# Making one more part of the first weights ahead of the first activation in a fused mLSTM and MLP kernel

## The chip, the cores and the metric

One NeuronCore of a Trainium2 chip runs the whole program; the other cores are idle. The metric is the device time of one execution in microseconds (us). Several executions of the same program are taken and their median is given.

## What is computed

The reference has two stages. The first is an mLSTM with 4 batches, 8 heads, 768 time steps and a head dimension of 40: a matrix state and a normaliser are carried along time with exponential input and forget gates, read out with the query, divided by a bounded norm and gated by a sigmoid. The second takes the result as 3072 rows of 320 features through an MLP with SiLU.

```python
h_tilde = np.einsum('bhde,bhe->bhd', C, qt)
denom = np.maximum(np.abs(nq), 1.0)
y[:, :, t] = o * h_tilde / denom
...
h = x @ w_in                      # [3072, 320] @ [320, 2048]
g = h * (1.0 / (1.0 + np.exp(-h)))
return (g @ w_out)                # [3072, 2048] @ [2048, 320]
```

The weights arrive as 64-bit floats.

## The kernel before, in words

**Units and steps.** Time is cut into 12 chunks of 64 steps and the batches into 2 pairs, which gives 24 units of 128 rows each. Three units make one step of the MLP (384 rows), so there are 8 steps (`Step`, L725). A step walks over 16 chunks of 128 hidden columns, `fc` = 0 to 15: `mm1(fc)` (L741) forms the hidden values in PSUM, `act(fc)` (L766) takes the tanh on ACT and the gate product on DVE, and `mm2(fc - 2)` (L797) adds to the three output tiles two chunks later (`LAG`). While one step runs, the attention work of the next three units is placed between its chunks: `block`, `close` and `turn` (L844 to L871) at the chunks given in `PLACES`.

**The weights.** They come in 20 parts (`Part`, L217), in the order that L319 writes out: c0 to c6 are tail weights (the last 64 input features, four chunks of columns each), i0 to i7 the other input weights (two chunks each), o0 to o7 the output weights (two chunks each). `load` (L225) issues one DMA on SP. `make` (L237) turns 64-bit words into 32-bit floats: two passes on ACT (L254, L255) and one on DVE (L256). `wmake(n)` (L331) makes the next n parts, and after each one issues the load of the next part not loaded yet. `halve` (L269) splits a tail part into a rounded part and a rest: two copies (L277) and two subtractions (L279), on ACT and DVE or, for c0, both on POOL. In step 0 `mm1(fc)` needs part i(fc // 2) and the halves of its tail part; its last two matmuls are those with the tail. `mm2(fc)` needs part o(fc // 2).

**What sets the order.** Each engine works through its own instructions in the order in which the program issues them. That order is written out by hand: a prologue (L896 to L983), then the chunks of step 0, each followed by the tuple of extra work in `FILL[fc]` (L984 to L1020). ACT, DVE and POOL take their shares of it in order, and SP issues its DMAs in order: eight hardware semaphores are used in turn, so a DMA waits until the eighth one before it has landed, and a load also waits until the buffer that it takes over was read for the last time (weights, q and k, and the rows of the MLP share the 11 buffers of the tag `big`).

**Around the change.** Before the first chunk the parts c0 and i0 are made, and c0 is halved on POOL. `FILL[0]` makes i1, adds the state of unit 2 (`state`, L659, matmuls), puts the states of units 1 and 2 into `Cm` on DVE (`carry`, L676: two copies L685 and two additions L693), finishes a part of the gates (L179, L180) and sends them to DRAM (`near`), and takes the exponent L422. `FILL[1]` makes o0 and takes the exponent of unit 3 (L393). `FILL[2]` makes i2, forms and weighs the scores of unit 3 (L523, L550), transposes gates (L194) and copies them (L204), loads unit 4 (v, k and o, D, lq), and prepares its mask on POOL (`shift`, L482). `FILL[3]` makes c2 and o1, halves c2 and adds the mask to D of unit 4 (L490); `FILL[4]` makes i3 and takes the exponent of D (L493); `FILL[5]` makes o2 and c4. At chunk 5 `block(3)` runs: unit 3 is read out, then normalised on DVE (L622 to L635) and scaled into `x` (L654); at chunk 6 `turn(3)` transposes it on PE (L709).

**PSUM.** The pool `psO` has three banks with the tag `o`. The states of units 1 and 2 (`pu`) and an exponent of unit 3 (`eq`) take them; the three output tiles of step 0 take them next, in `mm2(0)`. The hidden values use two banks of `psH`.

```python
order = "c0 i0 i1 o0 i2 c2 o1 i3 o2 c4 i4 o3 i5 o4 c6 i6 o5 i7 o6 o7"
def wmake(n):
    for p in parts[nmade[0] : nmade[0] + n]:
        p.make()
        wload(1)
    nmade[0] = min(nmade[0] + n, len(parts))
```

Of the kernel before, what the change touches and what calls it, by code (L numbers as in the profile page):

```python
# [43 lines left out]
def mlstm_mlp_kernel(  # L44
# [114 lines left out]
    def gates(lo, hi):  # L159

        init = NEG if lo == 0 else m_t[:, lo - 1 : lo]
        nc.vector.tensor_tensor_scan(
            m_t[:, lo:hi], f_t[:, lo:hi], i_t[:, lo:hi], init, op0=ALU.add, op1=ALU.max
        )
        yield
        l1 = max(lo, 1)
        tt = nc.vector.tensor_tensor
        tt(out=f_t[:, l1:hi], in0=f_t[:, l1:hi], in1=m_t[:, l1 - 1 : hi - 1], op=ALU.add)
        yield
        tt(out=f_t[:, l1:hi], in0=f_t[:, l1:hi], in1=m_t[:, l1:hi], op=ALU.subtract)  # L170
        nc.vector.tensor_scalar(f_t[:, l1:hi], f_t[:, l1:hi], -120.0, None, op0=ALU.max)
        if lo == 0:
            nc.vector.memset(f_t[:, 0:1], 0.0)
        yield
        nc.vector.tensor_tensor_scan(
            LF[:, lo:hi], pat[:, lo:hi], f_t[:, lo:hi], 0.0, op0=ALU.mult, op1=ALU.add
        )
        yield
        tt(out=i_t[:, lo:hi], in0=i_t[:, lo:hi], in1=m_t[:, lo:hi], op=ALU.subtract)  # L179
        tt(out=i_t[:, lo:hi], in0=i_t[:, lo:hi], in1=LF[:, lo:hi], op=ALU.subtract)  # L180
        yield
# [35 lines left out]
    class Part:  # L217
# [51 lines left out]
        def halve(self, eng=None, phases=(0, 1)):  # L269
            K, n, full = self.K, self.n, self.full  # L270
            for phase in phases:
                for k in range(2):
                    a, b = slice(k * K, (k + 1) * K), slice((1 - k) * K, (2 - k) * K)
                    cs = slice(k * n, (k + 1) * n)
                    hi = self.hi[a, :, cs]
                    if phase == 0:
                        eng.tensor_copy(hi, full[a]) if eng else nc.scalar.copy(hi, full[a])  # L277
                        continue
                    (eng or nc.vector).tensor_tensor(  # L279
                        out=self.hi[b, :, cs], in0=full[a], in1=hi.bitcast(F32), op=ALU.subtract  # L280
                    )
# [44 lines left out]
    def wload(n):  # L326
        for p in parts[nload[0] : nload[0] + n]:
            p.load()
        nload[0] = min(nload[0] + n, len(parts))
# [7 lines that stand above are left out]
# [536 lines left out]
    def run(n, it):  # L873
        for _ in range(n):
            next(it, None)

    u0, u1, u2, u3, u4 = units[:5]
# [29 lines left out]
    for _ in range(2):  # L907
# [5 lines left out]
    late = [gates(4 * L, 8 * L), gates(8 * L, S)]  # L913
# [67 lines left out]
    u2.xpose()  # L981
    u2.xput(st)
    u3.load_kvo()  # L983
    FILL = {  # L984
        0: lambda: (
            wmake(1),
            u2.state(),
            u1.carry(nc.vector.tensor_copy),
            u2.carry(),
            run(5, two),  # L990
# [2 lines left out]
        ),  # L993
        1: lambda: (wmake(1), u3.expo_act(), u3.near(), u4.load_qk()),
        2: lambda: (
            wmake(1),
            u3.scores(),
            u3.weigh(),
            run(2, near),
            u4.load_kvo(),  # L1000
            u4.load_d(),
            u4.load_q(),
            u4.shift(),
            u3.gate(),
            u3.keys(),
        ),
        3: lambda: (wmake(2), halve(2), u4.add(), run(1, late[0])),
        4: lambda: (wmake(1), u4.exp(), run(1, late[0])),
        5: lambda: wmake(2),
        6: lambda: (halve(4), wmake(2), run(1, late[0])),  # L1010
        7: lambda: (wmake(1), run(2, late[0])),
        8: lambda: (wmake(1), run(1, late[1])),
# [29 lines left out]
    for j in range(NSTEP):  # L1042
        st = steps[j]
        for fc in range(NFC):
# [28 lines left out]
            if j == 0:  # L1073
                FILL[fc]()

# [77 lines left out]
```

## Time and profile before

| | us |
|---|---|
| median of 3 runs | 451.97 |
| fastest and slowest run | 451.41, 453.16 |
| the profiled execution's own time | 454.21 |
| its span, from the first to the last instruction | 452.4 |
| PE busy (matmul) | 441.4 |
| DVE busy | 269.4 |
| ACT busy | 209.4 |
| POOL busy | 123.2 |

The profile is one execution taken by the hardware profiler. PE is the matrix engine (PEld its weight loads), DVE the vector engine, ACT the scalar engine, POOL the general engine, SP the engine that issues most of the DMAs (SPq its queue). A row of a timeline gives the start, the length, the engine, the line of the kernel, the operation, the output and the inputs by their names, their shapes and a count of merged instructions; in brackets stands how long the engine was idle before it and what released it. Matmuls are pipelined, so their lengths overlap a little.

### The profile page before, as it was taken

Reading aid. Unit: us, or ns where it says so; the run is one execution under the profiler, and the core shown is the slowest. Engines: PE = TensorE matmul, PEld = TensorE weight load, DVE = VectorE, ACT = ScalarE, POOL = GpSimd, SP = SyncE. Lnnn points to the kernel's source line nnn. Section 1 sums busy time; section 2 is a strip of 40 time slices with the busy share of each in tenths; the row PEclk is TensorE's granted clock in tenths of the full one; section 3 lists DMA queues with packets and bytes.
Section 4 is the critical chain, followed back from the end, with each engine's and each line's share of the span. In section 5 each row is a group of like instructions: output and inputs, shape, how many; then the busy total and the mean of one; then the engine's idle time right before and its main releaser. Section 6 shows DMA issues by size and latency. Waiting matters only on the chain.

```text
span 452.4 us, 11095 instructions
## 1 busy us (share of the span) xinstructions
PE 441.4 (98%) x4504; PEld 406.7 (90%) x4504; DVE 269.4 (60%) x595; ACT 209.4 (46%) x438; POOL 123.2 (27%) x134
## 2 busy tenths in 40 slices
PE   7989999999999999999999999999999999999996
PEld 4746577789999999999999999999999999999995
DVE  5765688768776655646646646646646555444442
ACT  7646456547446344354244354354354343334332
POOL 5821344222341322314323314313413230100000
PEclk9979999999999999999999999999999999999999
DMA  8999198414422514405403234315324110001001
GB/s 272 389 306 308 51 275 257 129 45 138 139 80 58 160 37 125 139 23 160 131 21 126 71 112 138 111 29 164 90 68 139 35 34 1 1 1 45 0 1 43
DMA packets 28691, 50.38 MB, mean 111 GB/s; under 512 B 3968, under 2 KB 15248, under 8 KB 28640
## 3 DMA queue, kind: packets, MB, share of 16 engines
q1 hardware_dynamic: 28288, 49.25, 35.2%
q8 instruction: 35, 0.57, 0.5%
q10 hardware_dynamic: 288, 0.34, 0.3%
q14 instruction: 16, 0.13, 0.1%
q0 software_dynamic: 64, 0.08, 0.1%
HBM read 45.65 MB, written 4.01 MB: 110 GB/s over the span
## 4 chain that ended last, share of the span: by engine, by line
PE 90%; DMA 5%; DVE 2%; ACT 1%; SPq 1%; issue 0%; ACTq 0%; DVEq 0%
PE ph L762 39%; PE pout L813 38%; PE p L609 3%; PE p L523 3%; PE pu L667 2%; PE p L594 2%; DMA wri<-in_w_in_dram 2%; PE p L709 2%; DMA vb<-in_vp_dram 1%; DMA qk<-in_qk_dram 1%; DVE wo L256 1%; PE pt L194 1%; SPq L438 0%; SPq L458 0%; SPq L235 0%
## 5 line engine op out<-in xcount | busy, mean ns | idle before, releaser
L769 ACT ACTIVATE th<-ph 128x384 f32<-128x384 f32 x128 | 62.5, 488 | 163.3 <-PE ph L762 160.9
L762 PE MATMUL ph<-xh,wh 128*128 128x384 f32 x336 | 115.4, 344 | 0.0
L783 DVE SCALAR_TENSOR_TENSOR th<-th,ph 128x384 f32<-128x384 f32 x112 | 62.1, 555 | 89.0 <-ACT th L769 88.4
L762 PE MATMUL ph<-xl,wh 128*128 128x384 f32 x336 | 113.7, 338 | 0.0
L813 PE MATMUL pout<-woh,gh 128*128 128x320 f32 x336 | 105.4, 314 | 0.0
L813 PE MATMUL pout<-woh,gl 128*128 128x320 f32 x336 | 103.9, 309 | 0.0
L813 PE MATMUL pout<-wol,gh 128*128 128x320 f32 x336 | 103.2, 307 | 0.0
L792 DVE TENSOR_TENSOR gl<-th,gh 128x384 fp32r<-128x384 f32 x112 | 65.6, 586 | 47.5 <-ACT gh L788 47.5
L788 ACT CAST gh<-th 128x384 fp32r<-128x384 f32 x112 | 57.5, 513 | 63.4 <-DVE th L783 62.7
L762 PE MATMUL ph<-xh,wl 128*128 128x384 f32 x224 | 75.9, 339 | 0.0
L813 PEld LDWEIGHTS pout<-woh,gh 128*128 128x128 f32 x336 | 63.0, 188 | 2.0
L687 POOL TENSOR_TENSOR Cm<-Cm,lq 40x328 f32<-40x328 f32 x40 | 30.1, 753 | 124.1 <-PE p L609 122.6
L762 PEld LDWEIGHTS ph<-xl,wh 128*128 128x128 f32 x336 | 63.1, 188 | 0.2
L762 PEld LDWEIGHTS ph<-xh,wh 128*128 128x128 f32 x336 | 63.1, 188 | 0.2
L813 PEld LDWEIGHTS pout<-woh,gl 128*128 128x128 f32 x336 | 63.0, 188 | 0.1
L813 PEld LDWEIGHTS pout<-wol,gh 128*128 128x128 f32 x336 | 63.1, 188 | 0.0
L507 POOL TENSOR_TENSOR qt<-qk,lq 104x512 f32<-104x512 f32 x22 | 29.2, 1326 | 121.5 <-ACT lq L503 114.9
L762 PEld LDWEIGHTS ph<-xh,wl 128*128 128x128 f32 x224 | 42.1, 188 | 0.0
L813 PE MATMUL pout<-wo,g 128*128 128x320 f32 x96 | 29.8, 448 | 2.9 <-DVE wo L256 2.9
L482 POOL TENSOR_TENSOR am<-mask,aT 128x512 f32<-128x512 f32 x20 | 24.3, 1215 | 9.3 <-DVE aT L204 7.8
L490 POOL TENSOR_TENSOR D<-D,am 128x512 f32<-128x512 f32 x20 | 25.8, 1289 | 2.2 <-DMA qk<-in_qk_dram 0.7
L550 DVE TENSOR_TENSOR D<-p,D 128x512 f32<-128x512 f32 x24 | 16.5, 689 | 16.3 <-PE p L609 11.3
(119 smaller groups left out, 494.9 us busy)
## 6 DMA issues: line engine op xcount, KB each, us to landing
qk<-in_qk_dram SPq DMA_DIRECT2D x24, 512.0 KB, 4.8
ko<-in_ko_dram SPq DMA_DIRECT2D x24, 320.0 KB, 4.5
wro<-in_w_out_dram SPq DMA_DIRECT2D x8, 640.0 KB, 7.0
D<-LFd SPq DMA_DIRECT2D x40, 128.0 KB, 3.1
lq<-LFd SPq DMA_DIRECT2D x40, 128.0 KB, 4.0
wri<-in_w_in_dram SPq DMA_DIRECT2D x8, 512.0 KB, 6.2
vb<-in_vp_dram SPq DMA_DIRECT2D x48, 82.0 KB, 4.5
out_dram<-ob SPq DMA_DIRECT2D x45, 80.0 KB, 2.1
```

What stands on the lines that cost most here:

```text
L482: nc.gpsimd.tensor_tensor(out=self.am, in0=mask.unsqueeze(1).broadcast_to([128, H, L]), in1=aT[:, self.c, self.p, :].unsqueeze(2).broadcas ...
L490: nc.gpsimd.tensor_tensor(out=self.Dm, in0=self.Dm, in1=self.am, op=ALU.add)
L507: nc.gpsimd.tensor_tensor(out=self.qt, in0=self.q[:KS], in1=self.lq[:KS], op=ALU.mult)
L523: nc.tensor.matmul(self.ps[d * L : (d + 1) * L, a * 4 + j, :], self.k[r, d * 4 + j, :], self.q[r, d * 4 + j, :], start=True, stop=True,)
L550: nc.vector.tensor_tensor(out=self.Dm, in0=self.ps, in1=self.Dm, op=ALU.mult)
L687: nc.gpsimd.tensor_tensor(out=v, in0=v, in1=self.lq[r, :, L - 1].unsqueeze(2).broadcast_to([D, H, D1]), op=ALU.mult,)
L762: nc.tensor.matmul(ph, w, x, start=(i == 0), stop=(i == len(ops) - 1))
L769: nc.scalar.activation(th, ph, AF.Tanh, scale=0.5)
L783: nc.vector.scalar_tensor_tensor(out=th, in0=th, scalar=1.0, in1=ph, op0=ALU.add, op1=ALU.mult)
L788: nc.scalar.copy(gh, th)
L792: nc.vector.tensor_tensor(out=gl, in0=th, in1=gh.bitcast(F32), op=ALU.subtract)
L813: nc.tensor.matmul(self.po[t], g[:, ts], w, start=(fc == 0 and i == 0), stop=(last and i == len(ops) - 1),)
```

## The change

One `wmake(1)` is put ahead of the tuple `FILL`, so that part i1 is made before the first chunk. The parts that follow stand one group earlier, up to o2: o0 in `FILL[0]`, i2 in `FILL[1]`, c2 and o1 with `halve(2)` in `FILL[2]`, i3 in `FILL[3]`, o2 in `FILL[4]`, c4 stays in `FILL[5]`. In `FILL[0]` the state of unit 2 goes ahead of the making, and in `FILL[2]` the scores and the weighing of unit 3 go ahead of it.

```diff
     u3.load_kvo()
+    wmake(1)
     FILL = {
         0: lambda: (
+            u2.state(),
             wmake(1),
-            u2.state(),
             u1.carry(nc.vector.tensor_copy),
...
         2: lambda: (
-            wmake(1),
             u3.scores(),
             u3.weigh(),
+            wmake(2),
             run(2, near),
             u4.load_kvo(),
             u4.load_d(),
             u4.load_q(),
             u4.shift(),
+            halve(2),
             u3.gate(),
             u3.keys(),
         ),
-        3: lambda: (wmake(2), halve(2), u4.add(), run(1, late[0])),
+        3: lambda: (wmake(1), u4.add(), run(1, late[0])),
         4: lambda: (wmake(1), u4.exp(), run(1, late[0])),
-        5: lambda: wmake(2),
+        5: lambda: wmake(1),
```

## Rows read from the trace of the kernel before

**Rows 1.** Busy time by stretches: stretch, length, busy (count) of each engine, clock, DMA.
```profile
60.00:70.00 10.00, 10.00 (x128) 7.45 (x127) 9.67 (x23) 5.02 (x11) 4.13 (x4) 1.00 0.99 287
...
300.00:400.00 100.00, 100.00 (x1057) 97.51 (x1056) 55.54 (x127) 41.64 (x88) 22.57 (x21) 1.00 0.20 60
```

**Rows 2.** Who waited for whom, 15 to 62 us: total, times, longest.
```profile
PE pout L813 <- DVE wo L256: 2.9, 2, 2.0
```

**Rows 3.** Timeline of PE, 20 to 80 us.
```profile
27.47 2.75 PE L813 MATMUL pout<-wo,g 128*128 128x320 f32 x6 [2.05 <-DVE wo L256]
...
39.20 0.62 PE L762 MATMUL ph<-xb,wh 128*128 128x384 f32 x2 [0.99 <-DVE wh L279]
...
49.73 1.88 PE L813 MATMUL pout<-wo,g 128*128 128x320 f32 x6 [0.85 <-DVE wo L256]
51.45 0.49 PE L709 MATMUL p<-ident,x 128*128 128x128 f32 x3
```

**Rows 4.** PE by half microseconds: stretch, length, busy (count), granted clock, DMA share, GB/s.
```profile
28.00:28.50 0.50, 0.50 (x3) 0.79 1.02 292
...
35.00:35.50 0.50, 0.50 (x4) 0.89 0.86 338
```

**Rows 5.** The chain that ended last, 27 to 62 us: start, length, what.
```profile
30.22 1.06 PE p L523 x32
...
31.85 3.46 PE ph L762 x6
...
57.16 1.61 PE pout L813 x6
58.78 1.64 PE ph L762 x6
60.42 0.62 PE p L523 x32
```

**Rows 6.** Timeline of ACT, 10 to 62 us.
```profile
21.13 0.49 ACT L769 ACTIVATE th<-ph 128x384 f32<-128x384 f32 x1 [1.82 <-PE ph L762]
...
24.10 0.80 ACT L254 ACTIVATE wro<-wro 128x640 f32<-128x640 f32 x1
24.79 0.75 ACT L255 ACTIVATE wro<-wro 128x640 uint32<-128x640 uint8 x1
...
35.34 0.49 ACT L769 ACTIVATE th<-ph 128x384 f32<-128x384 f32 x1 [7.47 <-PE ph L762]
...
41.57 0.61 ACT L493 ACTIVATE D<-D 128x512 f32<-128x512 f32 x1
```

**Rows 7.** Timeline of DVE, 10 to 62 us.
```profile
21.65 0.56 DVE L775 SCALAR_TENSOR_TENSOR g<-th,ph 128x384 f32<-128x384 f32 x1 [2.02 <-ACT th L769]
22.78 0.69 DVE L256 SCALAR_TENSOR_TENSOR wi<-wri 128x512 uint32<-128x512 uint32 x1 [0.57 <-ACT wri L255]
23.39 1.00 DVE L685 COPY Cm<-pu 40x328 f32<-40x328 f32 x2
24.40 1.00 DVE L693 TENSOR_TENSOR Cm<-Cm,pu 40x328 f32<-40x328 f32 x2
...
26.51 0.82 DVE L256 SCALAR_TENSOR_TENSOR wo<-wro 128x640 uint32<-128x640 uint32 x1
...
46.82 0.68 DVE L654 SCALAR_TENSOR_TENSOR x<-ko,p 128x256 f32<-128x256 f32 x3
...
48.46 1.21 DVE L256 SCALAR_TENSOR_TENSOR wo<-wro 128x640 uint32<-128x640 uint32 x1
```

**Rows 8.** Timeline of SP, 0 to 80 us: the issue of i1.
```profile
10.75 0.43 SPq L235 DMA_DIRECT2D wri<-in_w_in_dram  x1
```

**Rows 9.** DMA issues of SP, 10.7 to 11 us (i1): count, KB, us to landing.
```profile
wri<-in_w_in_dram SPq DMA_DIRECT2D x1, 512.0 KB, 5.9
```

**Rows 10.** Timeline of POOL, 0 to 62 us: the additions to D of units 4, 5.
```profile
33.84 1.27 POOL L490 TENSOR_TENSOR D<-D,am 128x512 f32<-128x512 f32 x1
...
47.72 1.28 POOL L490 TENSOR_TENSOR D<-D,am 128x512 f32<-128x512 f32 x1
```

## The prediction

> **What bounds the kernel now.** I read the busy time by stretches first: from 60 us to 400 us PE is busy for the whole of each of the eight stretches, so a microsecond that PE gets back before 60 us reaches the end of the program, unless a feeder of PE falls behind later [rows 1]. Next comes the list of waits between 15 and 62 us: PE waited for the making of output weights (the vector step of `make`, L256) twice, 2.9 us in all [rows 2]. The timeline of PE puts the places: 2.05 us before the first group of the second product (`mm2(0)`, parts o0), 0.99 us inside `mm1(4)` before its two matmuls with the tail weights (c2), and 0.85 us before `mm2(4)` (o2) [rows 3]. Last the granted clock in stretches of half a microsecond: PE runs at 2.4 GHz until it stands still, resumes, and then falls to 1.2 GHz, from 28.0 to 28.5 us on until between 35.0 and 35.5 us [rows 4]. The chain shows what that costs: the groups of 27 to 35 us take nearly twice what the same groups take later [rows 5].
>
> Why o0 is late is read on ACT and DVE, which work in the order of the program. o0 passes through ACT behind the tanh of chunk 1 [rows 6]; its step on DVE (26.51 us) stands behind i1, two copies and two additions of `carry`, and the gate of chunk 1 [rows 7].
>
> **The change part by part.** No instruction is added or taken away; seven parts and one `halve` change place.
>
> i1 ahead of the first activation: two ACT passes and one DVE pass. The passes on ACT took from the end of the first tanh (21.13 + 0.49) to 22.78, where DVE started: 1.16 us; DVE took 0.69 us [rows 6, 7]. Their cover is the hole before that tanh: ACT idle 1.82 us, DVE idle 2.02 us before the first gate [rows 6, 7]. 1.16 us fits ACT's hole, and DVE would end about 0.2 us before the gate is ready: cost nothing. The cover is gone if i1's bytes are late: issued at 10.75, landed 5.9 us later, 16.65 us; ACT is free for it from 21.13 - 1.82 = 19.31 on [rows 6, 8, 9]. Spare: 2.6 us.
>
> o0 one group earlier: ACT now gives it the place of i1, behind the tanh that ends at 21.62. Its two passes took from 24.10 to 25.54 us, 1.44 us, so they end near 23.1 [rows 6]; DVE needs 0.82 us, so o0 is ready near 23.9 instead of 27.33 [rows 7]. PE comes to `mm2(0)` at 27.47 - 2.05 = 25.42 us [rows 3]. **This stall, 2.05 us, goes.** What is late next there are the PSUM banks: the second and third tile of `mm2(0)` take the banks that the copies and additions of `carry` read, and these now stand behind o0. They took 1.0 and 1.0 us, from 23.39 to 25.40 [rows 7], so the copies end near 24.9 and the additions near 25.9; PE wants the second bank near 25.42 + 0.54 = 26.0 and the third near 26.5 (a third of 1.61 each). The banks are free in time, the third by 0.6 us.
>
> The clock: with no standstill at 25.4 us I take the fall to 1.2 GHz as gone. `mm2(0)` took 2.75 us [rows 3] against 1.61 in full clock, the scores of unit 3 took 1.06 against 0.62, `mm1(3)` 3.46 against 1.64 [rows 5]: 1.14 + 0.44 + 1.82 = **3.40 us**. The 0.57 us of small transposes between the scores and `mm1(3)` I leave out; halved they would be 0.28 more.
>
> c2, o1 and `halve(2)` one group earlier: in the kernel before, the tail was ready 39.2 - 35.34 = 3.9 us after the tanh that it follows [rows 3, 6]. It now follows the tanh of chunk 2, which comes near 25.9 us (PE ends `mm1(2)` at 25.42 and ACT still has i2 and the exponent of unit 3), so it is ready near 30 to 31, the weighing of unit 3 and the copies of `near` included. PE wants it after `mm2(0)`, scores, transposes, `mm1(3)`, `mm2(1)` and four matmuls of `mm1(4)`: 25.4 + 1.6 + 0.6 + 0.4 + 1.6 + 1.6 + 1.1 = 32.3 us. **The 0.99 us go.**
>
> o2 from group 5 to group 4: its DVE step took 1.21 us at 48.46, behind the chain of normalising unit 3, whose x was written from 46.82 [rows 7]. In group 4 it stands ahead of that chain, and several microseconds ahead of `mm2(4)`. **0.85 us go**, and the group that followed took 1.88 us where a fed one takes 1.61 [rows 3, 5]: 0.27 more.
>
> The DMA queue of SP: the order becomes o2, unit 4's q and k, c4, i4, then v, k/o, D and lq of unit 4. Two loads, 256 and 512 KB, pass ahead of those; at the 292 to 338 GB/s beside the clock rows [rows 4] that is 2.3 to 2.7 us for what stands behind. The one that matters is D: POOL added the mask from 33.84 to 35.11, ACT took the exponent at 41.57 [rows 6, 10], 6.5 us spare, and PE now arrives about 6.4 us earlier (2.05 + 3.40 + 0.99). So ACT may stand still for up to 2.7 us there. PE feels it only through the x of unit 3, written from 46.82 and transposed at 51.45 [rows 3, 7]: 4.6 us less its own 0.68, less the 1.12 of the o2 stall, leaves 2.8 us. Cost nothing, with little to spare at the worst end. Moving u2.state ahead of the making changes no engine's order, as one is all PE and the other has none: nothing.
>
> One contention has to be weighed. DVE's making of o2 took 1.21 us against 0.82 for o0, and POOL's addition ran from 47.72 to 49.00 over its first half [rows 7, 10]. The halving of c2 on DVE now falls where POOL starts the mask of unit 4. If POOL went first, the wait is at most one POOL addition, 1.28 us, and the tail would be ready at 32.3 at worst, just when PE wants it: I take no cost, 0.5 us as the bound. The Trainium skill, SBUF — State Buffer, section Who interferes with whom, says that a DVE instruction with two SBUF inputs and a GpSimd one that reads SBUF exclude each other, the second blocking fully; by that rule the order of issue decides here, and the 1.21 us row agrees with it only in part, since DVE is recorded as started before POOL ended.
>
> The sum: 2.05 + 3.40 + 0.99 + 0.85 + 0.27 = 7.56 us. The profiled execution took 454.21 us for a span of 452.4; by it the new one is 446.65. The median of the runs shown is 2.24 us lower, so I set the same gain against it: 451.97 - 7.56 = 444.41, call it **444.4 us**.
>
> **The rivals.** (a) The clock did not fall in the runs behind the median. For: the median is 2.24 us under the profiled execution. Against: the runs lie within 1.75 us, less than the 3.40 us at stake, so they are likely all of one kind, and the one trace has the fall. Then only the waits go: 451.97 - 4.16 = 447.8 us. The Trainium skill, TensorE: Matmul & The Clock Gate, Part 1, says the watch on PE's activity runs free of the kernel's start, so slow matmuls can differ between executions; no run here shows it.
>
> (b) A new wait in the old one's place: the banks of `mm2(0)`. For: o0's 0.82 us stands ahead of the carries on DVE now, and the third bank comes free only 0.6 us before PE asks for it. Against: every row from which that is worked out is a plain duration of this stretch. If the carries ended 1.5 us later, PE would stand about 1 us and, if the clock fell again, keep the 3.40: 444.4 + 1.0 + 3.4 = 448.8 us.
>
> (c) Slower: the exponent of unit 4 holds up ACT. c4 and i4 wait on SP for the buffers of i1 and o0, and D of unit 4 queues behind them. Each microsecond that D is later than 2.8 us beyond now costs one on PE, so the kernel gets slower from 2.8 + 7.6 = 10.4 us on; at 12 us it takes 453.6. Against: both buffers are released near 24 us, and the queue needs 2.3 to 2.7 us for the bytes.
>
> (d) One of the two later waits stays (the tail by the contention, or o2): 444.4 + 0.5 to 1.1, up to 445.5, inside the forecast's own range.
>
> **How the numbers follow.** Forecast with (d) 0.66, (a) 0.22, (b) 0.07, (c) 0.03, and 0.02 for no change. The range: below, the transposes (0.28) and, by my estimate, as much as 0.8 us of short restarts that the sum leaves out: 443.3. Above, to the upper edge of (a): 448.2. That leaves out (b), (c), no change and part of (a). A measurement of this kernel tells about 0.5% from no change, 2.3 us: faster means under 449.7. The forecast, (a) and (b) lie there: 0.95; no change 0.02, a late D that eats only the gain 0.01: 0.03 the same; the rest of (c) 0.02 slower.
>
> **What would show it.** Right: PE has no idle over half a microsecond between 24 and 50 us; the granted clock stays full through 28 to 35 us; o0's DVE step lies ahead of the carries, near 23 us; `mm2(0)` starts near 25.4 us and lasts about 1.6; unit 3's x is transposed near 44 us instead of 51.45. Wrong: a wait of PE for `carry` or its additions at 26 us; a clock of half between 28 and 35 us with no wait; ACT idle before the exponent of unit 4 for more than 3 us with PE idle behind it; or PE gaps after 60 us, which would say that the gain is given back later.

## The result and the profile after

The changed kernel takes 446.93 us (median of 4 runs, 446.67 to 449.48) against 452.57 us for the kernel before in the same comparison (4 runs, 451.41 to 453.43): a ratio of 0.989, interval 0.9846 to 0.9934. It is faster by 5.6 us where 7.6 was forecast (444.4 us); 446.93 lies inside the range, nearer to rival (a), 447.8, than to the forecast.

The profiled execution of the changed kernel is the slowest of the four: 449.48 us, span 447.7. Its timeline of PE answers to [rows 3] and [rows 5].

```profile
20.03 1.53 PE L762 MATMUL ph<-x,wi 128*128 128x384 f32 x4 [1.01 <-DVE wi L256]
...
25.93 1.78 PE L813 MATMUL pout<-wo,g 128*128 128x320 f32 x6
27.63 0.69 PE L523 MATMUL p<-qk 40*64 40x64 f32 x32
28.26 0.42 PE L194 MATMUL pt<-ident,home 32*64 32x32 f32 x8
28.61 1.56 PE L762 MATMUL ph<-x,wi 128*128 128x384 f32 x4
...
31.97 1.45 PE L762 MATMUL ph<-x,wi 128*128 128x384 f32 x4
32.97 0.81 PE L762 MATMUL ph<-xb,wh 128*128 128x384 f32 x2
...
42.67 1.78 PE L813 MATMUL pout<-wo,g 128*128 128x320 f32 x6
44.29 0.49 PE L709 MATMUL p<-ident,x 128*128 128x128 f32 x3
```

None of the three waits is left: `mm2(0)` at 25.93, the tail matmuls at 32.97 and `mm2(4)` at 42.67 follow their predecessors without a bracket. From the start of chunk 0 to the transposition of unit 3's x (L709) it is 44.29 - 20.03 = 24.26 us, where [rows 3] and the same start, 19.19 us, give 51.45 - 19.19 = 32.26. I call this length **the stretch**; all experiments are read on it. The granted clock stays full in it. By half microseconds, and then by stretches from 60 us on (columns as in [rows 1]):

```profile
28.00:28.50 0.50, 0.50 (x32) 0.43 (x23) 0.50 (x2) 0.50 (x2) 0.00 (x0) 1.00 1.04 410
...
35.00:35.50 0.50, 0.50 (x3) 0.34 (x2) 0.29 (x1) 0.50 (x2) 0.17 (x1) 1.00 1.11 260
```

```profile
60.00:70.00 10.00, 9.97 (x127) 7.28 (x126) 9.78 (x15) 7.39 (x14) 4.42 (x5) 1.00 0.96 291
70.00:80.00 10.00, 9.44 (x62) 6.73 (x61) 9.70 (x22) 5.16 (x10) 4.18 (x4) 1.00 0.53 146
80.00:90.00 10.00, 10.00 (x39) 7.70 (x38) 4.13 (x9) 3.50 (x7) 0.00 (x0) 0.83 0.08 26
```

Of the 8.0 us won in the stretch, about 2.5 went again between 70 and 90 us: PE is idle for 0.56 us, and behind it the clock is at half speed (1.2 GHz) from 80.4 to 83.9 us, 0.83 on average from 80 to 90. That is this one execution; the other three took 446.67 to 446.94. DVE in the stretch answers to [rows 7], POOL and ACT to [rows 10] and [rows 6].

```profile
23.82 0.83 DVE L256 SCALAR_TENSOR_TENSOR wo<-wro 128x640 uint32<-128x640 uint32 x1 [0.79 <-ACT wro L255]
24.56 1.00 DVE L685 COPY Cm<-pu 40x328 f32<-40x328 f32 x2
25.59 1.02 DVE L693 TENSOR_TENSOR Cm<-Cm,pu 40x328 f32<-40x328 f32 x2
...
30.77 1.59 DVE L279 TENSOR_TENSOR wh<-wtc,wh 64x256 fp32r<-64x256 f32 x2
```

```profile
30.93 1.15 POOL L482 TENSOR_TENSOR am<-mask,aT 128x512 f32<-128x512 f32 x1 [5.14 <-DVE aT L204]
35.33 1.28 POOL L490 TENSOR_TENSOR D<-D,am 128x512 f32<-128x512 f32 x1 [3.24 <-DMA D<-LFd]
```

```profile
36.64 0.63 ACT L493 ACTIVATE D<-D 128x512 f32<-128x512 f32 x1 [0.56 <-POOL D L490]
```

o0's step on DVE now stands ahead of the carries; the carries end at 26.61 us and PE does not wait for their banks. The halving of c2 takes 1.59 us instead of 0.87 beside POOL's mask, and ends at 32.36, 0.6 us before PE comes to it. D of unit 4 comes later (POOL waits 3.24 us for the DMA) and ACT stands still for 0.56 us.

### The profile page after: what moved, and what is told of

Its sections match the earlier page's. It is cut to its first block, busy times and chain, and to the rows that moved or that the text cites. A ratio compares the mean times of both kernels' runs of the same rounds, so it can differ in the third digit from the quotient of the medians.

```text
span 447.7 us, 11095 instructions
## 1 busy us (share of the span) xinstructions
PE 439.7 (98%) x4504; PEld 406.3 (91%) x4504; DVE 273.8 (61%) x595; ACT 209.6 (47%) x438; POOL 123.3 (28%) x134
## 4 chain that ended last, share of the span: by engine, by line
PE 87%; DVE 4%; DMA 4%; ACT 2%; issue 1%; SPq 1%; DVEq 0%; ACTq 0%
PE ph L762 39%; PE pout L813 37%; PE p L609 3%; PE p L523 3%; PE pu L667 2%; PE p L594 2%; DMA qk<-in_qk_dram 2%; PE p L709 1%; DMA wro<-in_w_out_dram 1%; DMA ko<-in_ko_dram 1%; DVE wi L256 1%; DVE wo L256 1%; DVE home L175 0%; PE pt L194 0%; DVE xl L721 0%
## 5 line engine op out<-in xcount | busy, mean ns | idle before, releaser
L762 PE MATMUL ph<-x,wi 128*128 128x384 f32 x64 | 24.1, 501 | 1.0 <-DVE wi L256 1.0
```

The lines of the kernel that those rows point to most:

```text
L762: nc.tensor.matmul(ph, w, x, start=(i == 0), stop=(i == len(ops) - 1))
```

## The experiments

Three runs repeat the two kernels as they are (e1, e2, e12). One fills the first wait of the kernel before (e4), four put parts of the change back (e5 to e8), and four try for more (e3, e9 to e11). The table has all kernels. "Full clock" are the executions whose mean granted clock is 0.998 or more; the stretch is that of the one traced execution. The median of the kernel before depends on how many of its executions lost the clock: over all timed executions it is 453.50 us, and the gain of the change 6.6 us.

| kernel | runs | median, us | at full clock: runs, median | stretch, us |
|---|---|---|---|---|
| before (with e1) | 67 | 453.50 | 28, 452.06 | 32.26; e1 30.64 |
| e4 standstill filled | 12 | 452.88 | 10, 452.29 | 29.78 |
| e5 only the front part | 10 | 449.94 | 8, 449.80 | 26.65 |
| e8 o0 late | 6 | 448.67 | 4, 448.38 | 25.77 |
| e7 tail late | 12 | 449.47 | 8, 448.22 | 25.52 |
| e6 o2 late | 6 | 448.11 | 5, 448.10 | 25.37 |
| after (with e2, e12) | 16 | 446.93 | 15, 446.92 | 24.26, 24.25, 24.25 |
| e3 | 6 | 446.99 | 6, 446.99 | 24.24 |
| e9 | 6 | 447.27 | 6, 447.27 | 24.25 |
| e10 | 6 | 447.30 | 5, 447.12 | 24.24 |
| e11 | 6 | 447.54 | 4, 447.24 | 25.79 |

**e1, the kernel before once more, no edit.**

> The kernel before, unchanged, to see the mean granted clock of every run. Theory: every run falls to 1.2 GHz after the standstill before the first group of the second product, as the traced one did (about 7 us at half clock, mean clock 0.99); times 451.4 to 453.5. Rival: the fall is in the traced execution alone, the timed runs show a mean clock of 1.00, and the gain of the change in them holds no clock.

453.04 us (12 runs) against 453.61 (23 runs of the same kernel), ratio 0.999, 0.9965 to 1.0016. Neither what was expected (every execution falls) nor its rival (only the traced one) holds. Its trace has the three waits at the same size, but the clock came back sooner. PE timeline, then PE by microseconds:

```profile
28.04 2.83 PE L813 MATMUL pout<-wo,g 128*128 128x320 f32 x6 [2.04 <-DVE wo L256]
...
38.16 0.62 PE L762 MATMUL ph<-xb,wh 128*128 128x384 f32 x2 [1.00 <-DVE wh L279]
```

```profile
28.00:29.00 1.00, 0.96 (x3) 0.70 (x4) 0.96 (x2) 0.46 (x2) 0.00 (x0) 0.89 1.00 258
29.00:30.00 1.00, 1.00 (x3) 0.67 (x2) 0.00 (x0) 0.00 (x0) 0.00 (x0) 0.50 0.90 212
...
32.00:33.00 1.00, 1.00 (x10) 0.79 (x11) 0.97 (x3) 0.00 (x0) 0.00 (x0) 0.91 1.04 311
```

Half speed lasts about 3.4 us here and about 7 us in the trace of before [rows 4], after the same wait. Each execution's mean clock shows which kind it was: the profile's list of cores gives, for before, e1 and e4 in this order,

```profile
core 0: 452.4 us, clock 0.991
```

```profile
core 0: 451.4 us, clock 0.996
```

```profile
core 0: 451.5 us, clock 1.000
```

So the 67 timed executions of the kernel before can be sorted by it, into three groups: 28 at 0.998 or more, median 452.06 us (450.97 to 453.86); 16 at 0.995 or 0.996, 453.52 (452.77 to 455.63); 23 at 0.994 or less, 454.93 (453.81 to 456.99). **The clock falls in 39 of 67 executions and stays full in 28, and a whole fall costs 454.93 - 452.06 = 2.9 us** (95% by resampling: 2.5 to 3.4). The mean does not say where in an execution the clock fell. That the place is the wait before `mm2(0)` is seen in the two traces; for the others it is taken over from them.

**e2 and e12, the changed kernel once more, no edit.**

> The changed kernel, unchanged. Theory: the timed runs lie at 446.7 to 447.0 with a mean clock of 1.00; the 2.5 us more of the traced execution are the fall of the clock at 80 to 84 us that follows the new wait of PE at 78 us, and come in some executions only. The start of the first chunk (20.03 against 19.19 us) varies with the landing of a load and is not the change's. Rival: the late start and the wait at 78 us are in every execution.

> The changed kernel once more, on the same chip as the three others, for comparison: 447 to 447.5 by the last time, and the stretch from the first chunk to the transposition of unit 3's x at 24.25 us by every theory. The start of the first chunk: 19.2 to 19.8 us if DVE's making of i0 starts ahead of POOL's subtractions, 20.0 to 20.8 if behind them.

447.39 us (6 runs, ratio 0.9866, 0.9832 to 0.9900) and 446.48 (6 runs, ratio 0.9857, 0.9825 to 0.9890). Fifteen of the sixteen executions of the changed kernel are at full clock. Neither trace has the 0.56 us wait or the half clock at 80 us. Where the first trace parts from e2's is this pair of rows on DVE and POOL:

```profile
65.61 1.43 DVE L171 TENSOR_SCALAR home<-home 32x256 f32<-32x256 f32 x1
```

```profile
65.60 1.30 POOL L507 TENSOR_TENSOR qt<-qk,lq 104x512 f32<-104x512 f32 x1 [4.49 <-DVE home L170]
```

DVE's instruction, started 10 ns after POOL's, took 1.43 us; in e2 it started 0.18 us ahead of POOL's and took 0.28. A second one followed, beside POOL's next row: the scan L175 took 1.22 us where e2's took 0.67. DVE has few holes there, so the last gates (L180) ended at 78.05 instead of 77.48 us and PE waited until 78.11, with the clock down behind it. That was in 1 of 16 executions, if the mean clock is taken as its mark.

In e12, D of unit 4 comes later than in the first trace, and ACT waits longer for it. Its rows on ACT and PE:

```profile
38.05 0.63 ACT L493 ACTIVATE D<-D 128x512 f32<-128x512 f32 x1 [2.03 <-POOL D L490]
```

```profile
20.01 1.53 PE L762 MATMUL ph<-x,wi 128*128 128x384 f32 x4 [0.99 <-DVE wi L256]
...
44.26 0.49 PE L709 MATMUL p<-ident,x 128*128 128x128 f32 x3
```

The stretch is 24.25 us all the same: 2.03 us of ACT cost PE nothing. In e3, where nothing in the stretch differs from the changed kernel, ACT waited 3.09 us, the most of all traces, and the stretch is 24.24.

**e4, the kernel before with its first wait filled with matmuls that no result uses.**

```diff
+            if j == 0 and fc == LAG:
+                warm(9, psU.tile([128, 512], F32, tag="u", name="fill"))
             if fc >= LAG and (j, fc) != (NSTEP - 1, NFC - 1):
                 st.mm2(fc - LAG)
```

> The kernel before with nine bf16 matmuls (128 x 512, into a free bank, results unused) put on PE between the first product of chunk 2 and the first group of the second product, where PE stood still for 2.05 us. All the waits stay. Theory: the standstill is what brings the clock down; without it PE runs at 2.4 GHz through 28 to 35 us, and the time is 3.0 to 3.6 us under the kernel before, about 449. Rival: the clock falls all the same, or had not fallen in the timed runs: 452 to 453, no difference.

452.88 us (12 runs), ratio 0.9988, 0.9961 to 1.0014. PE timeline and the clock in the place where before ran at half:

```profile
26.81 2.12 PE L890 MATMUL fill<-maskb,identb 128*128 128x512 bf16 x9
28.93 1.88 PE L813 MATMUL pout<-wo,g 128*128 128x320 f32 x6
...
35.08 1.45 PE L762 MATMUL ph<-x,wi 128*128 128x384 f32 x4
38.30 0.62 PE L762 MATMUL ph<-xb,wh 128*128 128x384 f32 x2 [1.77 <-DVE wh L279]
```

```profile
31.00:32.00 1.00, 1.00 (x41) 0.89 (x31) 0.50 (x1) 0.00 (x0) 0.00 (x0) 1.00 0.99 250
```

The fill takes the place of the wait, the clock stays full, and `mm2(0)`, scores and `mm1(3)` are at the short durations. But PE now comes earlier to the tail weights, which ACT and DVE have not moved, and waits 1.77 us for them instead of 0.99. So 0.78 us of what full clock gives are paid back at once, and the stretch is 32.26 - 29.78 = 2.48 us shorter than in the traced execution of before, near the 2.9 us (2.5 to 3.4) between the groups. The time near 449 that was expected did not come, since the median of the kernel before holds many executions that never lost the clock. At full clock e4 and before are alike (452.29 and 452.06); the fill makes full clock more frequent, 10 of 12 against 28 of 67. Two of the twelve fell all the same.

**e5, only the front: i1, o0 and i2 earlier; c2, o1 and o2 where they were.**

```diff
             u3.weigh(),
-            wmake(2),
...
-            halve(2),
...
-        3: lambda: (wmake(1), u4.add(), run(1, late[0])),
+        3: lambda: (wmake(2), halve(2), u4.add(), run(1, late[0])),
...
-        5: lambda: wmake(1),
+        5: lambda: wmake(2),
```

> Only the front of the change: i1 ahead of the first chunk, o0 and i2 one group earlier; c2, o1, the halving of c2, i3 and o2 back in their old groups. Measured from the start of the first chunk to the transposition of unit 3's x, which the changed kernel does in 24.25 us and the kernel before with its standstill filled in 29.78. Theory (each wait has its own price): the first wait and the fall of the clock stay away, the waits for the tail (1.0 to 1.8 us) and for o2 (0.85 and 0.27 us) come back: 26.4 to 27.2 us, 2.2 to 2.9 us slower than the changed kernel. Rival (one chain through ACT and DVE sets the pace, and the waits only hand the same loss on): the two later waits swallow the first one's gain, 29 us or more, 5 us slower than the changed kernel.

449.94 us (10 runs), ratio 0.9921, 0.9889 to 0.9953. PE timeline:

```profile
33.82 0.62 PE L762 MATMUL ph<-xb,wh 128*128 128x384 f32 x2 [1.00 <-DVE wh L279]
...
44.34 1.88 PE L813 MATMUL pout<-wo,g 128*128 128x320 f32 x6 [0.85 <-DVE wo L256]
46.06 0.49 PE L709 MATMUL p<-ident,x 128*128 128x128 f32 x3
```

The two later waits are back at the sizes of [rows 3]; the stretch is 26.65, 2.40 us more than after. The runs at full clock put it at 449.80 - 446.92 = 2.9 us (2.3 to 3.5 by resampling).

**e6, o2 alone late; e7, c2, o1 and the halving alone late; e8, o0 alone late.**

```diff
# e6
-        4: lambda: (wmake(1), u4.exp(), run(1, late[0])),
-        5: lambda: wmake(1),
+        4: lambda: (u4.exp(), run(1, late[0])),
+        5: lambda: wmake(2),
```

```diff
# e7
-            wmake(2),
...
-            halve(2),
...
-        3: lambda: (wmake(1), u4.add(), run(1, late[0])),
-        4: lambda: (wmake(1), u4.exp(), run(1, late[0])),
+        3: lambda: (wmake(2), halve(2), u4.add(), run(1, late[0])),
+        4: lambda: (wmake(2), u4.exp(), run(1, late[0])),
```

```diff
# e8
             u2.state(),
-            wmake(1),
             u1.carry(nc.vector.tensor_copy),
...
-        1: lambda: (wmake(1), u3.expo_act(), u3.near(), u4.load_qk()),
+        1: lambda: (wmake(2), u3.expo_act(), u3.near(), u4.load_qk()),
```

> The changed kernel with o2 back in group 5, made together with c4 behind the normalising of unit 3. Theory: the wait of 0.85 us before the second product of chunk 4 comes back and nothing else: 25.2 to 25.5 us on the same stretch, 1.1 us slower than the changed kernel. Rival: with the waits before it gone, PE reaches that group with the same lag to DVE and the wait is over 1.5 us, or it is hidden and under 0.3 us.

> The changed kernel with c2, o1 and the halving of c2 back in group 3 (i3 then stands with o2 in group 4). Theory: the wait inside the first product of chunk 4 comes back with 1.0 to 1.8 us: 25.3 to 26.2 us on the same stretch, 1.0 to 1.9 us slower than the changed kernel. Rival: i3 and o2 together in group 4 are late too, and the loss is over 2.5 us.

> The changed kernel with o0 back in group 1, made there ahead of i2; i1 stays ahead of the first chunk and all later parts stay early. Theory: the first wait comes back, shorter than before since DVE has the carries done sooner: 1.1 to 2.1 us; if it is long enough to bring the clock down, 0.9 to 3.4 us more: 25.4 to 29.7 us on the same stretch. Rival: the first wait was caused by i1's making on DVE and not by o0's place, and stays away: 24.3 us.

Ratios: e6 0.9885 (0.9838 to 0.9932), e7 0.9896 (0.9865 to 0.9927), e8 0.9892 (0.9849 to 0.9936). One row of PE each, in this order:

```profile
43.71 1.88 PE L813 MATMUL pout<-wo,g 128*128 128x320 f32 x6 [0.85 <-DVE wo L256]
```

```profile
33.71 0.62 PE L762 MATMUL ph<-xb,wh 128*128 128x384 f32 x2 [1.00 <-DVE wh L279]
```

```profile
27.42 1.85 PE L813 MATMUL pout<-wo,g 128*128 128x320 f32 x6 [1.28 <-DVE wo L256]
```

Each part brings back its own wait and nothing else. By the stretch, o2 is worth 25.37 - 24.25 = 1.12 us, the tail 1.27, o0 behind the carries 1.52; by the runs at full clock 1.18, 1.30 and 1.46 (448.10, 448.22 and 448.38 less 446.92; few runs, so each is known to about 0.7 us only). 1.12 + 1.27 = 2.39 is e5's 2.40: the two add up. Each wait costs about a quarter of a microsecond more than its bracket (1.12 for 0.85, 1.27 for 1.00, 1.52 for 1.28). In e8's trace the clock did not fall behind 1.28 us of standing still; two of its six runs, at 0.995, had a fall, but no trace shows where.

**e3, e9, e10, e11: attempts at more, on the changed kernel.** e3 moves the last transposes of gates (L194) one chunk later; e9 moves the subtraction that halves c0 from POOL to DVE, behind the last `xput` of the prologue; e10 is both; e11 lets the loads of unit 4 pass ahead of those of c4 and i4.

```diff
# e3
-        14: lambda: (units[8].load(), run(1, far)),
-        15: lambda: (run(1, far)),
+        14: lambda: units[8].load(),
+        15: lambda: run(2, far),
# e9
-    halve(0, nc.gpsimd)
+    halve(0, nc.gpsimd, (0,))
...
     u2.xput(st)
+    halve(0, None, (1,))
# e11
-            wmake(2),
             run(2, near),
             u4.load_kvo(),
             u4.load_d(),
             u4.load_q(),
+            wmake(2),
```

> The changed kernel with the transposes of the last gates on PE put one chunk later (after the second product of chunk 13 instead of chunk 12), so that PE reaches them after DVE has made their input. Theory: the new wait at 78 us (0.56 us) is gone and with it the fall of the clock behind it: 0.4 to 0.8 us under the changed kernel's undisturbed runs, near 446.3, and no run with the 2.5 us more. Rival: the wait is only moved (the copies behind the transposes now hold up DVE and PE at the start of step 1), and the time stays at 446.9.

> The changed kernel with the two subtractions that halve c0 moved from POOL to DVE, behind the last rest of x. Theory: DVE's making of i0 (0.69 us when it starts ahead of POOL's subtractions, 0.99 to 1.22 us and 0.3 to 0.8 us of waiting of PE when it starts behind them) waits for POOL; without POOL's subtractions it takes 0.69 to 0.72 us, PE waits less than 0.7 us before the first chunk, and the time is 0.3 to 0.8 us under the changed kernel. Rival: the late start comes from the landing of unit 2's k and o alone, the making of i0 is long all the same, or DVE has no room for 0.87 us more there: no gain, or a loss.

> The same, and the transposes of the last gates one chunk later. Theory: 0.3 to 0.6 us under the one before it, since the wait that the traced execution of the changed kernel had at 78 us, and the fall of the clock behind it, can't come. Rival: that wait was rare, and the two are the same.

> The changed kernel with c2 and o1 made after the loads of unit 4 are issued, so that the loads of c4 and i4 stand behind unit 4's v, k, o, D and lq on SP again. Theory: POOL's addition to D of unit 4 comes 1.5 to 2.7 us earlier and ACT's wait of 0.56 us before the exponent goes, but PE never felt it: the stretch from the first chunk to the transposition of unit 3's x stays at 24.2 to 24.3 us and the time is that of the changed kernel. Rival: ACT's wait delayed PE, and the stretch is 0.3 us or more shorter.

None gains what was expected of it: 446.99 (ratio 0.9855, 0.9826 to 0.9884), 447.27 (0.9866, 0.9831 to 0.9900), 447.30 (0.9869, 0.9836 to 0.9902) and 447.54 us (0.9892, 0.9853 to 0.9931), against 446.93 over all runs of the changed kernel. e9 was to give DVE a free run at i0 (its vector step took 1.22 us in the trace after and 0.72 in that of before). It did not, since the next work of POOL stood there instead; DVE, then POOL of e9:

```profile
19.73 1.01 DVE L256 SCALAR_TENSOR_TENSOR wi<-wri 128x512 uint32<-128x512 uint32 x1 [0.47 <-ACT wri L255]
```

```profile
19.45 1.89 POOL L687 TENSOR_TENSOR Cm<-Cm,lq 40x328 f32<-40x328 f32 x2
```

e11 did what it was to do for D, and as expected it is worth nothing: ACT no longer waits before the exponent (39.21 us, no bracket), and PE has no wait behind chunk 0, as in e12 where ACT waited 2.03 us. Its stretch is longer only through the clock, which fell behind the wait for i0. PE timeline and PE by microseconds of e11:

```profile
21.77 2.10 PE L762 MATMUL ph<-x,wi 128*128 128x384 f32 x4 [1.44 <-DVE wi L256]
```

```profile
23.00:24.00 1.00, 1.00 (x4) 0.67 (x2) 0.57 (x1) 0.00 (x0) 0.93 (x2) 0.50 1.01 326
```

At full clock e11 takes 447.24 us, 0.3 more than after, within the noise. No version is shown to beat the changed kernel.

## Why the prediction was right, and where it was off

**The waits: right in place, a little short in price.** Chunk 0 started 0.84 us later in this execution than in that of before; that has to be taken off its times. o0's vector step came at 23.82 (23.1 forecast), the banks were free in time, `mm2(0)` took 1.70 us to the next group, and x was transposed at 44.29 (near 44 forecast; less 0.84 it is 43.5). The halving of c2 met POOL's mask as feared and ended at 32.36. Less 0.84 that is 31.5, later than the 30 to 31 of the text and before its worst case, 32.3; PE did not wait. The sum counted the cost of a restart once, 0.27 us; e6, e7 and e8 show it behind each of the three waits, so some 0.5 us were missing.

**i1 and the loads: cost nothing, as said.** Chunk 0 starts at 20.03, 20.36 and 20.01 us in the three traces after, at 19.19 and 19.76 in those of before, but at 20.77 in e4, in which nothing was moved up, and at 19.41 in e5, in which i1 was. Each of these starts waited for i0's vector step or for x, which stand ahead of i1 in the program, so the spread comes ahead of the change. For D, ACT stood still for 0.52 to 3.09 us (up to 2.7 allowed), and the stretch is 24.24 to 24.26 us in six traces that keep the clock full in it, e3's with the 3.09 among them.

**The clock: right for the traced execution, wrong for the median.** In an execution with the fall the changed kernel gains 454.93 - 446.92 = 8.01 us (7.45 to 8.67), and the two first traces differ by 8.00 in the stretch; the sum with three restarts instead of one, 7.56 + 0.54 = 8.1, agrees. The term of 3.40 us was somewhat large: it set 2.75 us, a length of the timeline, against 1.61, one of the chain, where a fed group has 1.78 in the timeline. From `mm2(0)` to `mm2(1)` PE took 35.14 - 27.47 = 7.67 us in the trace of before and 31.93 - 27.42 = 4.51 in e8's, which has the wait and full clock, so the clock cost 3.16 us there. The rows of `mm2(1)`, before and e8:

```profile
35.14 1.78 PE L813 MATMUL pout<-wo,g 128*128 128x320 f32 x6
```

```profile
31.93 1.78 PE L813 MATMUL pout<-wo,g 128*128 128x320 f32 x6
```

The step that failed is "The median of the runs shown is 2.24 us lower, so I set the same gain against it". Those 2.24 us were in the main the fall itself: two of the three runs shown, 451.97 among them, lie below 452.77, the fastest of the 39 executions with one. (The clock of these three is not on record.) Set against its own execution, the sum gave 446.65 us; 446.92 was measured at full clock. That they lie so close is in part luck, since executions with a whole fall spread from 453.81 to 456.99 us.

**Rival (a) was told right and weighed wrong.** The argument against it was that the runs lie within 1.75 us and so are of one kind, the kind of the trace. By their times two of them were of the other kind; 453.16 can be of either. And runs within 1.75 us need not be of one kind: the kinds differ by 2.9 us and not 3.40, since the tail wait takes a part back (e4), and a fall of about 3.4 us costs only 453.52 - 452.06 = 1.5. Its own figure, 4.16 us, missed that too: where the clock does not fall, the tail wait to be removed is 1.77 us and not 0.99, as e4's trace has it. 2.05 + 1.77 + 0.84 and three restarts of 0.27 make 5.5; the stretches give 29.78 - 24.25 = 5.53, the groups at full clock 452.06 - 446.92 = 5.14 (4.63 to 5.62).

The Trainium skill, TensorE: Matmul & The Clock Gate, Part 1, says that the watch on PE's activity does not start with the kernel, so that the same kernel shows different numbers of slow matmuls from run to run. The prediction said that no run here shows such differences; the 67 executions now do, in three groups. Whether that watch is what makes them was not tried.

**The other rivals.** (b) and (c) did not come: no wait for the banks, no PE wait behind the late D. (d) did not come either. That a gain could be given back after 60 us, a sign of being wrong in the prediction, came true in one execution of the changed kernel, by a wait of 0.56 us at 78 us that the prediction had not named.

## What to carry to other kernels

Before the price of a fallen clock goes into a sum, sort the timed executions by their mean granted clock and set the sum against an execution of the same kind: a trace with the fall and a median without it differ by that price. Where a stall or a slow clock goes, work out anew what the next late part then costs, since PE comes to it earlier (here 0.78 us of 3.40 went back into the tail wait). And count a restart, here about a quarter of a microsecond, for each wait removed.

## What the runs showed that was not expected

**The length of a wait does not tell whether the clock falls.** The same wait before `mm2(0)`, 2.05 us, was followed by about 7 us of half speed in the trace of before and by about 3.4 us in e1's, and by the mean clock 28 of 67 executions had no fall at all. 1.28 us (e8), 1.33 (e9), 1.36 (e10) and 1.77 (e4) were followed by none in their traces, 1.44 us (e11) by some 3.4 us of it, and in the trace after 0.56 us, between two groups of 32x32 transposes (0.65 and 1.37 us), by 3.4 us too.

**DVE's lengthened instructions.** Where DVE loses time to POOL, the profile shows no idle, but a longer instruction: 0.28 us became 1.43 (L171) beside the POOL row that began 10 ns before, and the two subtractions of c2 took 1.59 instead of 0.87, ending 0.28 us after POOL's mask. A bracket of PE that names DVE has then to be followed to the DVE row whose mean is too long. The Trainium skill, SBUF — State Buffer, section Who interferes with whom, says that one of DVE's pairs of ports is shared with POOL as an exclusive lock, and that the order of issue decides which one blocks. Both rows agree with it, and e2's, with the order turned round and 0.28 us, does too. By the same section not every DVE instruction takes the shared pair; that L171, which has one input, takes it is read here only from its length.
